# A new static order for one fused kernel: the first convolution block ahead of the second on every queue

## The chip, the cores and the metric

One NeuronCore of one Trainium2 chip runs the whole program. The metric is the device time of an execution in microseconds (us); smaller is better.

## The reference

```python
# x = A_q (2048 x 640), k = A_k, v = A_v
q   = layernorm(x)
ks  = sum over t in 0..3 of k shifted down by t rows * shift_k[:, t]      # a short causal filter
kv  = ks * v
y   = causal convolution of kv with ssm_k over the 2048 rows, per column  # by FFT, length 4096
h   = x + q * (y + kv * ssm_D)
z   = layernorm(h)
out = h + (silu(z @ w_gate) * (z @ w_up)) @ w_down      # 640 -> 1728 -> 640
```

All inputs and the output are bf16.

## The kernel before

**The work.** The 2048 rows are cut into four blocks of 512 rows, `j` = 0 to 3, and the 640 columns into two halves of 320, `c` = 0 and 1. Per block there is a convolution part and a feed-forward part. A convolution of length 1024 between blocks is done as matmuls with constant tables. For each block and half:

- `kvm`, `kva`, `kvv` (VectorE, L501): the four taps and the product with v.
- `s1X`, `s1K` (TensorE, L492): the first transform step of kv and of ssm_k, four groups `b` each, evacuated as `e1X`, `e1K` (L475 on ScalarE, L476 on VectorE).
- `shX`, `shK`: four transfers from SBUF to SBUF that regroup the partitions; they need all four `e1`.
- `s2X`, `s2K`: the second step, four groups `G`, evacuated as `e2X`, `e2K`. In block 0 three of the four spectra come in one dense step from a table of 1 MB (`full`) and need no `s1`, no `sh`.
- `swB`, `swX`, `swC`: transfers that swap even and odd partitions of a spectrum, two issues each.
- `mr`, `mi`, `ar`, `ai` (VectorE, L501): complex products of spectra, 1280 columns each. Block j uses the spectra of the blocks before it as well.
- `i2` (TensorE), `e3` (ScalarE L478 or VectorE L479), `rs` (transfers), `i1` (TensorE): the inverse. `i1` needs all four `rs` of its half.
- `o`, `h` (VectorE) and `q` (L777 on VectorE, L778 on ScalarE): the gate and the residual sum; then batch statistics `bn`, `ag` (L755, L759), `va` (L766), a power on GpSimd `nr` (L768) and `nm` (L770) for the second layer norm, in two pairs of row tiles.
- `hn`: the normalised rows; turned by TensorE in block 0 (`tr`, L988, evacuated by `te`) and by transposing transfers in the others (`hx`, L981).

Feed-forward: `gu` is a group of five matmuls of 512 columns (each of four groups in block 0's first pair as two of 256); `si` and `ue` on ScalarE (L1034, L1050) and `gm` on VectorE evacuate a pair; `dn` is the down projection, three groups for each of four row tiles; `fa` adds the residual and `st` stores.

So `s2K10G1` reads: second step, K, block 1, half 0, group 1. In `i1011` the step is `i1`, then come block 0, half 1 and row pair 1.

**The order.** All 1,219 operations are collected in a list. A table `_ORDER`, compressed and written into the source as text, gives each an engine and a start time, made offline from fixed costs per operation. `replay` sorts by these times and so fixes, for each of the five queues (TensorE, ScalarE, VectorE, GpSimd, SyncE "SP"), which operation follows which; `emit` then adds the semaphore waits. Each queue is worked in order. On the chip nothing waits for a start time, but the times have three more effects: rotating buffers are handed out in their order; the gaps that they leave on TensorE before the first `gu` are filled with matmuls of 192 columns on zeros (the fillers, L515, `o.lead`), one for each 0.083 us (0.166 in the first 6.9 us); and a transfer that would have nothing to wait for is tied to the last operation that ends before its start.

```python
gap = o.start - end - 0.25
o.lead = max(0, int(gap / 0.083)) if o.start > cold else max(0, int(gap / 0.166))
```

**Buffers that matter here.** PSUM has four tiles of two banks: `pF` (two) and `pC` (two); block 0's convolution uses both kinds, later blocks `pC` alone, and feed-forward `pF`. `H` (between `e3` and `rs`) has two buffers, `HT` (between `rs` and `i1`) one, `PP` (products) three, `KIN` and `VIN` one each. The weights `wg3`, `wg9` and others go into space that the table `full` had.

The memset `gpad` (`P.warm`) zeroes what the fillers read.

Of the kernel before, what the change touches and what calls it, by code (L numbers as in the profile page):

```python
# [1126 lines left out]
_ORDER = (
    "c-pO030PBC7A7x`kdOtkhwLj^$i4sx*~tb3LLh`B2#6?%vRJFFindy}X>Bc4i+qk&#tpYBE|t1f9c|UNRIS#PDq2NtYf-0)wiPG1b!_X@nXmV}@0|0_yZ4-X"
    "{`=ntfDi~2h=Dv101AQ+ofrrRg+M_F2!g;<1Ny{!v?eOi0Y3J@fe!=rsX+8CS|?^;*(3A&EKepr$4cnH3*^y$qG1pUjcz^qfDa5b=Fxyafafz&JzxOvH|k+p"
    "=(8~Rb*~`!4F7SPPj&WG6nNCi<CgwBIq>|+A%Bp30KJE^9(sQbQs9FzKnCD}dKOB+A2#)$jCcUbQ|x%=gkRfwUhMv~B=CQfjN%A9Mils~5Pity=Rowo@a|dU"  # L1130
    "co+vj$m1p;{~Lb5?+O5qejC4u1AoXr;0gbtr5>UM{HcBxPD^4UF)JaFm;qS?xdN$z@PP_|2|Ws70+sPCG2cU+z*t~DZ~?%BI`DWb1@<AN4^|IpM7g1#K@Y@)"
    "AR@@Su|2UII0|f!<Hvp!TM8D#uE1YMyoTsS-bT_<+tI^;4FC*U58Vr$4xRxqus$FH{SsuvB4Wd_T~HL*2X%vIW0%D?!M=kB;-<#M!>7Xc!kvimu%BUK#A!rx"
    "{I&SiNG^(xtVeD|DiKo<Y4KI@Juo*s2tNtm5Z{Dyqb{S==t*cMx*ok9U6Y_mIE&em5W=p-9mMWQ>`QFJ+`vx5y+b;OuY!4Fcfhc5)o~}|vf+#2TyQFQBX(C@"
    "ZfpSNMRX#zB9_EAz(=F^qF=!5z#tR*6S5NLB{sw%;RW%%@%xd3P!VJgQjZj)M<wpZl5v%|d)NZpIoxdAQT%OuKH(cefH;x39P1=ZBJL;FkhYSpl9mxS5V0f*"
    "X%gu?$wj_RT1mb|9zu?gH<GuJ&yh<g4U{&DFlkKEJxmvA5<W~_OJBeik&tW{OV8RT=w{Cn9TFWBy&-8%dV%^fC4*X?1X8zAI+J!%ebkw>9NIoAg1(k+rb`*k"
    "%#T=KbB;4;tWxemRu{KlP$BH)mk7=a>y!PW@k|QiJ8l;DF0+<*m-jJG#qSiJN-h_y7nO)5Y$zunTEl*ubCz>lBolukX_QvUa#df;7RvLLe)S%;RdGP^qjIcj"
    "s``j{M~XpqL_SNk1cr&P1PQ1%v@BsV;uNYEGlv2}Yccl|P?$+b7`2)X#qJ?rV|UQMrVr)n5!d1GAb9cT;<d;X$bRI@apSOOuu4oH=5S&S_7>WL5#Z+F|AAxR"
    "C!u@Lqfp0C0rYBg5vm2H#H_{CV>%Ot<6H0(2_1xK37ZmhiPIBz6TeJE5;JgYQVsbS?jZR(B_nA@5}PuT0#Ntk;|Ws2M8dp88TJ#xZNdS9gSeP_g=(hlOxjKf"
    "Qafk>y^B7UzMD>EjN@+QuHgK_q3~Yk>G%qvfe-Q*@vrcmf-M4Ja!Yb4W(9_vP?sP~+?JStos2z<XOl*fwvgtNgQPanb|Q>qrS40rr*Ecdar<xpQB7Qgi^1E7"
    "qlhojjHH`1CH)5)gRZ2N)21;tGgeY5v=F18v5O969$^k;-DY{&vw5TVSNS2{0iIBBn47};fZNNBVHL5KvhJ|P@;>5}@|UqU@#_S?@XrcblVQRm!V$@zCeIbV"  # L1140
    "B1Ve)M0Rnv*e}tf?2(j8Orj=9w`5t$MCmo@dKpnlmyVUzN#{z5vhU?@$XXPO<svypK3P6q{+_&2L02{@<|v8EpR}{J2K5)J3A*iSK`KZ4fo6ZICT)rKXqrkd"
    "*Zfm$PyZ@yo#v+gvSD|IK7(LhX}V~9*DSV1Qa{vvZWwI%HnlN>Yr2@eM9;IVvE&)n*)(>e=@ny#In#XHL^Ch5Fzl~p@*JS+kmrJ9gj4K-dC*xkR-p}-33rq_"
    "I$g8e*`8j{xojM^pIk;BLD|S+ayDppqz_7+lBP(P=(F{Bqt(=7xNahuTg|!nW_%oB0U>$?DPR(s`U<s~UC0^5+0E%>Q#gwmy^K1(fqRZyB)r6=vh2*!%u?q2"
    "%$Y0=dkuf7V3;6IykF2KIL7A-E(kQqPT|<-O}N2J5cMScl8c2`g>Q*);#T2&F<dfEGCk$1l!-E5%7T=ODW9h-lYT3qDoRrLQoZO!(H8L~ak;cz%9Q2FVr2G|"
    "ZL*UxhD<5{n|!3=o?^42P`O4KqpDD?RmG&vSCKTjv|TEh<_pa#?O^R(-Om=4^;=_{xzXBbZLq^LH(GC5-Nsc$hV8fwY45i0rPb5nj55Y1hL`z1%fvY^*e&8n"
    "u1HVI+GHeoSh7q~A&)4WYPw>Iyj{*$1QZVG80j$idBs6hf+|jZUwujmSM5|fR0}kE-3oQT_Pkc7ou<2}hO1xFbm>;70%;Ygp|tk2*z|Sj7=4?$R^Jgl!TISP"
    "!+rgGh7U5_M!$ZG9%EQ-kQ(cZ%QH@7+%jxU?J)8(YBTyXVl5F%lkt?X%v5ZC-+aSrw9T-otxK)ftPWeDv)i)K^_Fdndz{T_Uv9r{w`PvXJeS##>31y5?6ONU"
    "8y)Qqg7c!I)-lF`aypzf&d;6QQF+sq;L33tow=@K&b!VEm*2h0HN%Z?AMy?HHRPSin~`7PyPZES2bD9^+njqRr#g@1qj@p8Tm0Gnw{zbt$O<0ySh6zm+ww`-"
    "R)1Q-)WY6EZBc8{Yk@;SOR+lpldPWLgkVL^{9<H?Txcpd5a=tcEkp-q7P&(ohjSx`BB;88;=`d(SQPo9c6;QrlC08COW9?aC4oU*gGx)w%9b;IiosH@w8T0&"
    "ZG=~wzc=qfJ~7YjUsQO~uPzV;t^_bedy9T#zssR<=W;E)cHZCBH?<}WKXqN|;<PF0RXS&y#9+<Pm@b*OSza(rG2bvR)E(DxObbj4%~DIM^^RqyGsX6{WtW9)"  # L1150
    "t+wuW+;+enX^wq1n{%f--?PGVBI{>Yde-bLcJ^1<f}Hl8#o1T0wK*79o$IDk<?8TU_7FUo9-^l*yC$2K1A4>WCEjg0cf7f|K;9i+W`26!)Vy8!DaF%+C4r=("
    "#^UwG?$9^ICyGuK%?X?haDuJDW5Ic0vNl_nm)@OTr*AXOx7WDVn|f>$?ai*ATulzOv)vYNAD#1#N9XIyD{^<aN4Z<wYqHK{DLk)w1ld32Ov#se|K;W8-p>hm"
    "FXl9PC*-cqZOpr$+nE=W*Xq0FGv^ok=H>hRs|tQBI1%VBP!<x4@ctIR+`rJzEqJlO?c3qI=08yIgFm^jvCv$!uP`gHIB+X~4i*QO1T%wkgWbV<!HVM3#e&e-"
    "(5etDd^WT;bRmQdRfOc>Vc{L&OX1RRFpQ4872X)05Sbm7oe@I`Cz2GQl#GtFM4|^+(qGb1q8+5IY^~fmOkBkoy1MFm#k7j%DxiAQkk_iK%V(F7E7lCYT;5WF"
    "9y)%gYxu_DcZX_fEQ61hpRTU2-Zi*n_@E&NhWLkF8tSS1au~O4OX*K#OUqKrCYCjpvuZZgY#nK+ZK}-}v2TQTWamh3ZCc%~y3O^e4YL}OYuDAf>krm58~zP&"
    "9!w_"
)


# [26 lines left out]
```

## Time and profile before

| | |
|---|---|
| median of 11 runs | 312.33 us (307.07 to 315.2) |
| the profiled execution, its own time | 313.62 us |
| its span, first to last instruction | 311.8 us |
| TensorE, VectorE, ScalarE, GpSimd busy | 285.3, 235.0, 187.4, 27.0 us |
| mean granted TensorE clock | 0.986 |
| instructions | 4,974 |

A busy TensorE here includes the fillers, and a matmul's record is longer than the interval at which the next follows, since matmuls are pipelined. So busy time says how long the engine was not empty, and not how much work was done.

### The profile page before, as it was taken

To read this page: it belongs to the slowest core of one execution; us is meant where nothing else is said; L and a number is where in the kernel's file an instruction comes from. 1 tells how busy PE (TensorE), PEld (TensorE's weight loads), DVE (VectorE), ACT (ScalarE), POOL (GpSimd) and SP (SyncE) were. 2 spreads that over 40 slices of the span, in tenths; PEclk is the share of its full clock that TensorE was granted. 3 is DMA by queue.
4 is the path that set the end of the run, shared out by engine and by line. 5 is a ranking of instruction groups with operands and counts; after the bars stand their busy time and mean duration, and the time that the engine had idled before them with its cause. 6 is when DMAs were issued, how large, how long until landed. Compare 5 with 4: busy or idle time off the path is not lost.

```text
span 311.8 us, 4974 instructions
## 1 busy us (share of the span) xinstructions
PE 285.3 (91%) x1765; PEld 169.1 (54%) x1780; DVE 235.0 (75%) x406; ACT 187.4 (60%) x280; POOL 27.0 (9%) x34
## 2 busy tenths in 40 slices
...
GB/s 226 330 168 308 147 210 252 201 204 276 216 301 240 299 266 298 151 273 191 211 288 9 137 182 126 113 163 181 214 113 84 44 43 84 2 0 0 2 84 43
DMA packets 53116, 52.09 MB, mean 167 GB/s; under 512 B 21202, under 2 KB 46163, under 8 KB 53092
## 3 DMA queue, kind: packets, MB, share of 16 engines
...
q10 hardware_dynamic: 1010, 0.79, 0.7%
q8 instruction: 14, 0.23, 0.3%
q14 instruction: 10, 0.08, 0.1%
...
## 4 chain that ended last, share of the span: by engine, by line
PE 60%; DMA 15%; DVE 10%; ACT 7%; SPq 4%; issue 3%; POOL 0%; ACTq 0%; DVEq 0%
PE ps L492 56%; DMA sb<-sb 11%; DVE sb L501 8%; SPq L483 3%; ACT sb L475 3%; PE ps L515 3%; DMA sb<-in_A_ssm_k_dram 2%; ACT sb L778 1%; DMA sb<-in_A_q_dram 1%; DVE stt L755 1%; ACT sb L478 1%; ACT sb L790 1%; PE ps L624 1%; DVE sb L777 1%; POOL stt L768 0%
## 5 line engine op out<-in xcount | busy, mean ns | idle before, releaser
L492 PE MATMUL ps<-sb 128*128 128x320 bf16 (+3 forms) x1113 | 207.9, 337 | 2.7 <-DVE sb L501 1.5
L501 DVE TENSOR_TENSOR sb<-sb 128x1280 bf16<-128x1280 bf16 (+2 forms) x238 | 174.2, 768 | 17.3 <-PE ps L492 6.1
L492 PEld LDWEIGHTS ps<-sb 128*128 128x128 bf16 (+2 forms) x1128 | 109.0, 98 | 83.9 <-issue 5.4
L475 ACT ACTIVATE sb<-ps 128x640 bf16<-128x640 f32 x131 | 88.7, 712 | 39.0 <-PE ps L492 38.0
L492 PE MATMUL ps<-sb,tab 128*128 128x320 bf16 x450 | 79.8, 308 | 10.5 <-DMA sb<-sb 6.5
L492 PEld LDWEIGHTS ps<-sb,tab 128*128 128x128 f16 x450 | 42.9, 100 | 38.9 <-DMA sb<-sb 8.1
L501 DVE TENSOR_TENSOR sb<-ps,sb 128x640 bf16<-128x640 f32 (+3 forms) x34 | 29.2, 858 | 42.2 <-PE ps L492 40.4
L1034 ACT ACTIVATE sb<-ps 128x1024 bf16<-128x1024 f32 (+2 forms) x32 | 29.3, 916 | 23.7 <-PE ps L492 23.5
L478 ACT ACTIVATE sb<-ps 128x640 bf16<-128x640 f32 x31 | 21.1, 705 | 12.7 <-PE ps L492 12.6
L778 ACT ACTIVATE sb<-sb,stt 128x320 bf16<-128x320 bf16 (+1 forms) x34 | 24.0, 729 | 7.4 <-DVE stt L770 4.8
L515 PE MATMUL ps<-sb 128*128 128x192 bf16 x158 | 20.0, 275 | 7.7 <-ACT sb L475 4.9
L755 DVE BATCH_NORM_STATS2 stt<-sb 128x6 f32<-128x320 bf16 x48 | 22.3, 485 | 0.2
L1050 ACT ACTIVATE sb<-ps 128x1024 bf16<-128x1024 f32 x18 | 18.4, 1024 | 6.0 <-PE ps L492 5.1
L515 PEld LDWEIGHTS ps<-sb 128*128 128x128 bf16 x158 | 14.6, 108 | 13.2 <-ACT sb L475 7.9
L768 POOL TENSOR_TENSOR stt<-stt 128x2 f32<-128x2 f32 (+1 forms) x10 | 11.4, 1138 | 52.8 <-DVE stt L766 42.4
L476 DVE CAST sb<-ps 128x640 bf16<-128x640 f32 (+1 forms) x8 | 6.2, 780 | 9.1 <-PE ps L492 9.1
L804 POOL TENSOR_TENSOR stt<-stt 128x4 f32<-128x4 f32 x2 | 2.6, 1296 | 77.8 <-DVE stt L802 77.8
L790 ACT ACTIVATE sb<-sb 128x640 bf16<-128x640 bf16 x8 | 6.0, 744 | 2.4 <-DMA sb<-in_A_q_dram 2.4
L797 ACT ACTIVATE sb<-sb,stt 128x640 bf16<-128x640 bf16 x8 | 6.6, 832 | 0.0
L777 DVE TENSOR_SCALAR sb<-sb,stt 128x320 bf16<-128x320 bf16 (+1 forms) x14 | 5.5, 395 | 0.9 <-DMA sb<-sb 0.5
L483 POOL DMA_DIRECT2D sb<-in_B_w_down_dram x3 | 2.1, 698 | 33.1 <-DVE sb L501 29.1
L483 POOL DMA_DIRECT2D sb<-in_A_k_dram x2 | 2.1, 1028 | 27.8 <-DVE stt L759 27.8
...
## 6 DMA issues: line engine op xcount, KB each, us to landing
...
```

Source lines behind the costliest of these rows:

```text
L475: fns = {"act": lambda a: a.activation(out=dst(), in_=src(), func=ACTF.Copy), "dve": lambda v: v.tensor_copy(out=dst(), in_=src())}
L478: fns = {"act": lambda a: a.activation(out=dst(), in_=src(), func=ACTF.Copy, scale=scale), "dve": lambda v: v.tensor_scalar(out=dst(), in0 ...
L483: fns = [(lambda g, d=d, s=s: g.dma_start(d(), s())) for d, s in subs]
L492: return lambda t: t.matmul(o(), l(), r(), start=st, stop=sp)
L501: return lambda v: v.tensor_tensor(out=o(), in0=a(), in1=b_(), op=op)
L515: P.fill = lambda t, pt: t.matmul(B32(pt, 1, 192), V(GUT, 13 * 512 + 256, 128), V(GUT, 13 * 512, 192), start=True, stop=True)
L755: vec(dve1(CW, False), lambda v: v.bn_stats(st6(l, j, b, c), V(xt, b * D + c * CW, CW)), [(xt, (b, c))], [(ST, ("s", j % 2, b, c))], prio, ...
L768: P.op({"pool": 0.95}, lambda g: g.tensor_tensor(out=y, in0=va, in1=stt[:, 288:288 + hi - lo], op=ALU.pow), c1 + [(ST, "half")], c3, prio, ...
L778: "act": lambda a: a.activation(out=dst(), in_=src(), func=ACTF.Identity, scale=rs(l, j, b), bias=tmv(l, j, 3)[:, b:b + 1])},
L790: P.op({"act": act_c(D) + 0.22}, lambda a, b=b, jt=jt: a.activation(out=V(jt, 0, D), in_=V(xt, b * D, D), func=ACTF.Copy, accum_out=tmv(l, ...
L1034: P.op({"act": act_c(n)}, lambda a: a.activation(out=dst(), in_=src(), func=ACTF.Silu), rd, wr, -1000, name=f"si{j}{i}")
L1050: P.op({"act": act_c(1024)}, lambda a: a.activation(out=V(ut, 0, 1024), in_=B32x2(u, 512), func=ACTF.Copy), [(u, 0), (u, 1)], [(ut, 0)], - ...
```

## The change

The table is replaced by another; costs, operations, tiles and pools stay as they are. Besides, `replay` puts the memset `gpad` first on its queue (before, the memset `wpad`, 0.33 us, came first).

```diff
@@ -126,6 +126,11 @@
                 tl.left -= 1
                 if tl.left == 0 and tl.pool is not None:
                     self.pools[tl.pool].free.append((max(p.finish for p in tl.touch), tl.base, tl.touch))
+        q = self.order[self.warm.eng]
+        q.remove(self.warm)
+        q.insert(0, self.warm)
+        for i, o in enumerate(q):
+            o.pos = i
 
         end, cold = 0.6, 6.9
@@ -1125,35 +1130,34 @@
 _INFO = None
 _ORDER = (
-    "c-pO030PBC7A7x`kdOtkhwLj^$i4sx*~tb3LLh`B2#6?%vRJFFindy}X>Bc4i+qk&#tpYBE|t1f9c|UNRIS#PDq2NtYf-0)wiPG1b!_X@nXmV}@0|0_yZ4-X"
...
+    "c-pm730PBC7EWGPLKYGdLLhrW_JwSOY-Aw|Ss)}35)uU2Q3R!Kt#un)t75Ao)rt#R>8G{sj*41w7qw2uqS$KdI$CS(xK?YeI(CBEs%`z+nXhy1cJ6uS{^#8P"
...
```

Decoded, the two tables differ as follows (`xN` for N groups in a row; a convolution group is named by step and block alone). TensorE, from the sixth group of `s2K0` on to the first feed-forward groups:

```
before: ... i20x2 s2X0x2 s1X1x2 i20x2 s1X1x2 s1K1x2 i20 i10x2 s2X1 i20 s2X1x2 s1K1x2 i20x2 s1X1x2 s2K1x2 i10
        s2K1x2 s2X1 s1X1x2 i10 s1K1x4 tr00 i21 gu0x2 i21 tr01 gu0x6 s2X1 gu0 s2K1 gu0 i21 ...
after:  ... i20 s2X0 i20 s2X0x2 i20 s1X1 i20 s1X1x3 i20 i10 i20 i10 s2X1 i20x2 s1K1x3 i10 s1K1 i10 s2X1x3 s1X1
        s2K1 s1X1 s2K1 tr00 s2K1 gu0 tr01 gu0x4 s1X1 gu0x3 s1K1 s1X1 gu0 s2K1 gu0 s1K1 gu0 ...
```

Of block 1, `s2K10G2`, `s1X11b1`, `s1X11b3`, the four `s1K11` and `i210G1` stand ahead of the first `gu` before, and behind it after. On VectorE, thirteen instructions of the products and taps of blocks 1 and 2 and of statistics stand ahead of the second `nm` of block 0 before and behind it after (`mr1000`, `mr1001`, `mi1000`, `mi1001`, `ar1001`, `ai1001`, five of `kvm20` and `kva20`, `bn0130`, `ag013`); six come ahead of it (`he01`, `q013`, `bn0110`, `ag011`, `hn00`, `hn01`). SP begins `taps kin0 kraw00 x0 kraw01 full vin0 tab1` before and `taps kin0 kraw01 kraw00 full vin0 x0 tab1 shK00G0 tab2 kin10 swB000` after. The weights `wg3`, `wg9` and `wu3` are issued by GpSimd before, and after by SP, in the order `swB100 wu3 gul1 wg9 wg3 wu9`. 17 operations move from ScalarE to VectorE and 16 the other way; 22 transfers change their queue. At the end, TensorE has `i13x2` and eleven `dn2` ahead of the last stage before, and after `i13`, two `dn2`, `i13` and nine `dn2`. The last stage itself (27 `gu3`, 12 `dn3`) differs in the order within it. The fillers are 158 before and 176 after.

More of the change, by code (lines that the diff above doesn't have):

```diff
@@ L1127 @@
 _ORDER = (
-    "c-pO030PBC7A7x`kdOtkhwLj^$i4sx*~tb3LLh`B2#6?%vRJFFindy}X>Bc4i+qk&#tpYBE|t1f9c|UNRIS#PDq2NtYf-0)wiPG1b!_X@nXmV}@0|0_yZ4-X"
-    "{`=ntfDi~2h=Dv101AQ+ofrrRg+M_F2!g;<1Ny{!v?eOi0Y3J@fe!=rsX+8CS|?^;*(3A&EKepr$4cnH3*^y$qG1pUjcz^qfDa5b=Fxyafafz&JzxOvH|k+p"
-    "=(8~Rb*~`!4F7SPPj&WG6nNCi<CgwBIq>|+A%Bp30KJE^9(sQbQs9FzKnCD}dKOB+A2#)$jCcUbQ|x%=gkRfwUhMv~B=CQfjN%A9Mils~5Pity=Rowo@a|dU"
-    "co+vj$m1p;{~Lb5?+O5qejC4u1AoXr;0gbtr5>UM{HcBxPD^4UF)JaFm;qS?xdN$z@PP_|2|Ws70+sPCG2cU+z*t~DZ~?%BI`DWb1@<AN4^|IpM7g1#K@Y@)"
@@ L1132 @@
[L1132 to L1155, printed above, removed]
@@ L1156 @@
-    "9!w_"
+    "c-pm730PBC7EWGPLKYGdLLhrW_JwSOY-Aw|Ss)}35)uU2Q3R!Kt#un)t75Ao)rt#R>8G{sj*41w7qw2uqS$KdI$CS(xK?YeI(CBEs%`z+nXhy1cJ6uS{^#8P"
+    "o(Dj|U<d#LKWYF33I+9V;sXi=L!j{)3Opx}pS34v;w=vGRPX-)ebj$pi2L*(d$Rln$`i+*4d7p%1VGPb0RlhOAo0Ze1p<ZicL?Z-#4-NZ@+cSx1VDc=^<zR_"
+    "%)!%J#^ty5pRV~FC(l{IPp;B`^Jl|6eu}4nz;och9|Q;g8XOYeJ@$I6{V7aA9x(-pmjW1gH2qgBL7%M%=%ZqIwmM$u0Dxb_-Ty7*?=cz={^u|XeN@!{E2Gb+"
+    "{v!KN`~iQMzsCdt&j0~02mm}+f53BW0l#7k_}%$MJaqt3kT5>_TL<_mxDLD?JQs*T4g=MY5V{@oHP``+1S)}*z+~wAP&Z5i-vWLJy9A6#VnA4s2>3226{tiW"
@@ new lines @@
+    "MUIEhPN+h+qvj(*aC<^4T8!ah9M~A<FPO8~BS0Et6$F5Wp`SoAU}Ioz$P&mJs2<h^-2)v2eF*&$Iuf=Eb|1z^?1udt-ho()IE$Ez9G;Mhcz_fl;V3_9YT}7R"
+    "4*DWWlQ<!<2&qlbBG)DyLims<)SIY_sD#9mXeDMG<{;*E%qN&M?7y)?acEp0t}E#>9#4=YElzp`XT#6KuORdh_QKHcW$^p(0Add!6*&$07K8w;fwjOVB`{Fw"
+    "i5-a&^lJ1V)CSB0OgC1A+lkA?Eydlyjf7VsuE18ocP3s&zl{0;H5J*E)QY>G<ioe)dy<myQT%QE4*W{OeL^5Pk2pDb3Z9QIPJWm?jChI&CAAa3Pgavw5swh_"
+    "NM)o6Bw@;^6bZ>dT0we`bdXe*GA!lo6ghb;`5b01?pP{@9A->mY$HP{5Q2$(m^+ML#BLKBMVEx1l0QyuAfr?7rj(~HBF{-(N;#LBoi-_rn|_KCqAX26nl_4B"
@@ new lines @@
+    "NS{qRkp3>Um(HRgnDyL7-mHx4+yQ(7Z=&E1Gm|-w^%7$=%fs%<n8AUu*YPp@H11*HE23_?fVPQ!fw6@)iJ|4>32%yZ(oUIA#gU(vzmbVh98{f>E|A^IoUg#D"
+    "Od_RtjHFh2LU9$|k+2jALa)K|2`3YD1Qli%egm-@b2HIRo{s5G^^<5xiz)Z08B{OzJk6VMAGtkY7b=*zJduKKLsz0l5_S^K6Qs#-LLH$OFCuJ8zLm^M8J#=`"
+    "lZY+BPR6!jcViD?T-XByPy9tc!(SuOQijJ_d!4wEs7k6%YDf{1Hm88d7|MvWWt2l{D(ZM@1${8}8(If_HwBc|kaCsWn*3ohjHo7h)0UE?)b&&ZZ62+VHkN*m"
+    ";b6{WE@WO}x>>ilG)9Ee$#G=d%n0!xifS{|oZ~z;KO*QBj1ppH`Pg@`SFlzbH|b1LC1Fjnf;cPvWV$!)owRFdx^xJ|n8u<js8d+0sf&p>h`Fi5Q)iOSl5~_o"
@@ new lines @@
+    "l%doEX%}d)^fQc!Of|iR4x+2*7}_}6KbR-!=b6XoaCSR;1nV06VMa5L$5-=K@M`#dTw%sr>~6M^(a30F-(`=;uyMxlx;be6IR0K9PH<E}6SfKG3jQf57PbqI"
+    "i+V&!;-TVmVxq((St9a@w~67B?ULJ)F6kL*mt>9PisYgMC0!%kCk@EBGMXGNn;=^tdt0_urjgH=yX6^~%jNS_Fm<c)j`9ulWffSnKdUs$t7%a?wSU*NX1}AL"
+    "E6cKvX;&yuXLsvLOiK-)7$rt)j^7ltD78m52eTV>x3%T^Cc`B?MvpX)FxMM8EmN)XoINJ8rP{nOXS8{)Mc`cLEOzzeo%9qqPPrE3McfzMH!O#&LEDzx3Xdcg"
+    "VV`N=>|l95Pp+YKQdUrxvu3fkt2?z<vbO2`*?sz6^Ci>aoUz6kmJJrFwS}CVvM;rSa-EW#-jMzc?O)Vb#<C0+=L|=|9m~DP+02#kZe)DTn=j~Na#&%;`;02q"
@@ new lines @@
+    "QPy}Cmi>UUgY$!En}{m#3C8e2f;s$se2K73ctS9QXBK@akO~(GdE&X^%=jO-NmMJLN^4|mWpu?dDM{9*ydta2%#ulzM)_g6S1?sTljchg$nVGpXU@;;%v>T%"
+    "QIa!PWCj!$6eE>L)ehwV)h1P<`m|c0QD+e~HJXpJtJPc7?`iI8tXWiTlXa|hLC$RRe(OZr6gxS$#b&S_$>E!~*{<6-j^Pd+V+SLb+0GQRwzK@~;hauBLR2ey"
+    "Aetn;B$+1d6^caj6=e#$x>fb6qFK30uFQlemCAvNnF_eNSNT%bB=vaJYE_lWq28?dAS)-UIcr_k7L7z3)%0c6YS(D3**)2JwduOyy1TkD`h9whd7U0)7;bLW"
+    "FE?-v2IEb`=SIBIVk|QJXxL~ZnA(k>8K)ZyvtKj))yOt&G&Pz~ISX@&a%AR><^;=D3)K3N^)-vdI^Ei5(b~+pUpW`KGV?auuG;R{thuvt0egi#%f2PI&fc3V"
@@ new lines @@
+    "vahq>w<Dci$2t26`$ETUJH@fi@r9$#sdMgknw((g4Cfr@HmBV6sw>xZ-Sv{Iq;Q=7yMk#2kiaN^d!WtB^U?~&<WKf3D!}@0`3ilJU{CN+{@|jEA+vkGdrzS!"
+    ";PPAuGzS+I9SL-Y{GnK}v1Dt>hn@mYQy3i9d#{D}L{=ADiv=a)L-^2=(3tSPQeX7bXi4m1`RC#G2($Ey(t-iI%JK&E4hWXNUv7&XiUrG#m7Q)Pu@lrI#ai(u"
+    "`vcu8zV(Hi!g~cr{j^|G(dOc=;Qk_Ss3mkdgyaUe%eW7?O&Jv4etv7#F7<I8Tfa!F)2Ve6bj^mn288KH6UyQ+t+oDWwPr8LzHhFx7)&coZd;Fy=a^zUXBJsD"
+    "<zCO#xg>eJT{m4i`-(iAdu-kkH^STD1bf1sLT|SZk$<(|q1Wx}@U3)z;l?;OJ8Sc1=RL45a)iD0Zg0M-U}}Ne59IIg%+9}@&nO&O$O&Hd&ktM-RD{#RsA5~F"
```

4 lines of the change are left out of this document (added).

## The prediction

> **What bounds the kernel now.** I read the busy times by stage first, cut where the first matmul of each feed-forward stage starts and where the last convolution ends (columns: stretch, length, busy time and count of TensorE, weight loads, VectorE, ScalarE, GpSimd, then clock, DMA share, GB/s):
>
> ```profile
> 0.00:77.00 77.00, 63.62 (x447) 40.90 (x448) 57.17 (x106) 48.45 (x72) 12.43 (x19) 0.96 0.75 231
> 77.00:262.00 185.00, 177.60 (x1078) 104.52 (x1091) 165.29 (x289) 131.58 (x200) 14.53 (x15) 1.00 0.57 178
> 262.00:306.30 44.30, 44.09 (x244) 23.67 (x244) 11.75 (x13) 7.33 (x8) 0.00 (x0) 1.00 0.07 23
> ...
> 77.00:255.20 178.20, 170.93 (x1030) 99.87 (x1042) 163.22 (x285) 131.58 (x200) 14.53 (x15) 1.00 0.58 181
> ```
>
> Two resources are nearly full between 77 and 255 us: TensorE, and VectorE with 163.2 of 178.2 (15.0 idle). After 262 TensorE runs the last feed-forward stage alone. The slack lies ahead of 77, and there the busy figure misleads, because of the fillers:
>
> ```profile
> L515 PE MATMUL ps<-sb 128*128 128x192 bf16 x158 | 20.0, 275 | 7.7 <-ACT sb L475 4.9
> ```
>
> Next the issue rate. The last stage is 135 matmuls of 512 columns and 112 of 320 by the code, and takes 306.23 - 261.76 = 44.5 us by the chain of waits: 0.216 and 0.136 us each fit. At these rates (0.056 for a 128-column transpose) all 336 TensorE groups are 257.9 us of work. The last one ends at 306.2, so 48.3 us are not work. Ahead of the first feed-forward group, which ends at 77.7, lie 36.8 us of work with it: 40.9 of the 48.3 us are lost there. Only 7.5 us are lost later.
>
> Then the chain of waits and TensorE's timeline, to see what the front waits for:
>
> ```profile
> 26.51 0.61 SPq L483
> 27.12 0.04 issue
> 27.16 5.67 DMA sb<-sb
> 32.83 0.02 issue
> 32.86 0.84 DVE sb L501
> ...
> 60.89 5.21 DMA sb<-sb
> 66.10 0.05 issue
> 66.14 0.46 PE ps L492 x2
> ```
>
> ```profile
> 66.14 0.45 PE L492 MATMUL ps<-sb,tab 128*128 128x320 bf16 x2 [2.59 <-DMA sb<-sb]
> ...
> 74.92 0.73 PE L988 MATMUL ps<-sb 128*128 128x128 bf16 x10
> ...
> 76.98 1.26 PE L492 MATMUL ps<-sb 128*128 128x256 bf16 x10
> ```
>
> The pair at 66.14 is `s2K10G1`, of block 1. It stands in TensorE's queue ahead of block 0's last inverse group `i1011`, so block 0 waited for block 1's 5.2 us shuffle: `i1010` ended at 63.05, `i1011` only at 69.94. That is what the change takes apart. The transposes at 74.92 (`tr00`) and the first feed-forward matmuls follow from it.
>
> **What the Trainium skill says.** "TensorE: Matmul & The Clock Gate", Back-to-back issue gap: N/2.4 + 2.5 ns, so 215.8 and 135.8 ns; the stage above agrees within 0.5%. The same page's table of specifications gives ScalarE and VectorE a strict first-in-first-out queue: an instruction that waits holds all behind it; VectorE's 2.33 us before 67.36 is such a wait. "DMA: Bandwidth & Descriptors", Issuing engines are not separate DMA queues: moving a transfer between SP, ACT and POOL saves issue time alone, so I price the ten or so transfers that change queues in the front at their 0.4 to 0.6 us of issue. Its Anatomy of one DMA gives 2.0 us plus bytes over 436 GB/s, 2.4 us for 160 KB. The page's median for these shuffles is 2.3 us, but on the chain they take 4.7 to 5.7; I use those.
>
> **The change part by part.** No arithmetic is added; each operation keeps its size.
>
> *TensorE ahead of the first feed-forward group.* Seven groups of block 1 (`s2K10G2`, `s1X11b1`, `s1X11b3`, four `s1K11`) and `i210G1` move behind it: 26 matmuls of 320 columns, 26 x 0.136 = 3.5 us. Work with that group falls from 36.8 to 33.3. Fillers rise from 158 to 176 (18 x 0.083 = 1.5 us); they stand in front of groups that wait for data anyway and are free while that wait lasts, at most +1.5.
>
> *The front's chain*, old ends against mine:
> - Loads. `x0` goes behind `full` and `vin0`, and both `ktr` run together. The pair `s2K00G0/G1` lies at 10.4 us of work instead of 11.4 and `ktr01` waits for nothing. I put `e2K00G1` at 23.5 (before 26.15). The swap `swB000`, two issues of 0.6 and 5.7 us, lands at 30; `mi0000` ends at 30.7 (before 33.7).
> - `mi0010` follows after eleven VectorE instructions, 6.5 us: 37. `i200G3` ends at 38.3 (before 42.2), its evacuations at 39.8, the `rs00` transfers (0.6 each, 4.5) land at 44.5; `i1001` 45.6 (before 46.9).
> - HT and the two H buffers are single file: `rs01` can't start before `i1001` has read HT. `i201G2` then ends near 48.5 (before 56.3, held by `mi0110`, which came behind outputs and taps on VectorE); its evacuations wait for H until 51.5; the last `rs01` lands at 56.
> - `i1010`, `i1011`: 56.1 and 57.2, with nothing of block 1 that waits between them (before 63.05 and 69.94).
> - VectorE: `o010` to the first `nm10`, 17 instructions, 5 us: 62.0, the GpSimd power of 1.2 us beside the batch statistics. Then `hn00`, `hn01` on VectorE (0.45 each), 63.1; second half 65.1.
> - Ahead of `tr00` TensorE still has `s2K10G1` and `s2K10G0`, whose shuffles are issued after `e1K10b1` (57.3) and land at 63 to 64. So `tr00` 65, `te00` (1.2 us on ScalarE) 66.3, first feed-forward group **67** instead of 77.7.
>
> TensorE's loss at that point: 67 - 33.3 = 33.7 instead of 40.9, 7.2 us won.
>
> *Beside the first feed-forward stage.* New costs: weight piece `wg3` was on GpSimd, issued at 60.0; now it is on SP behind `swB100`, `wu3`, `gul1` and `wg9`: about 2 us of issue after `e2K10G0`, plus 4.6 us landing, near 73.5. `gu011` needs it after 6.6 us of work, at 73.6: 0 to 2 us, I take 1. VectorE's `e1X11b1` (behind four half-groups on TensorE) costs VectorE up to 3 us near 68.
>
> TensorE's bound for the last stage: 67 + (213.4 - 33.3) work + 7.5 + 1 = 255.6, against 261.7: 6.1 won.
>
> *VectorE's bound.* Thirteen instructions of blocks 1 and 2 (8.8 us) are behind the second `nm10`'s place now, six others ahead of it. By its own intervals VectorE has done 51.4 us when the second normalisation begins, instead of 57.7; from there to the last `nm13` the new order has 171.1 us, the old one 162.7 (2 us of the difference are evacuations taken over from ScalarE). So 64.6 + 171.1 + idle. Idle was 15.0; a reason to gain: block 0's chain no longer interrupts; a reason to lose: more to do beside feed-forward evacuations. Bounds 11 to 20; I take 16, with `e1X11b1` in it: 251.7. From the last `nm13` (255.2) to the landing of the last `hx3` took 5.2 us before: 256.9.
>
> *The end.* After `i1311` nine groups of the third down projection remain, instead of eleven: 11.4 us of cover, 13.9 before. The chain below it (`y`, `o`, `h`, statistics, power, `hn33`, two transposing transfers of 1.23 us issue, 2.4 landing) was 12.4; with `hn31` earlier I make it 10.5. It fits by 1 us; if not, 1 to 2 us go back.
>
> The later bound counts: 256.9 against 261.7, **4.8 us** won, on the profiled execution 313.6 - 4.8 = 308.8. That execution lay 0.4% above the median of 312.33; in the same ratio, 312.3 x 308.8/313.6 = **307.5 us**.
>
> **The rivals.**
> - *VectorE gives nothing back* (no change). Idle of 20 us cancels it: 64.6 + 171.1 + 20 + 5.2 = 260.9. For it: VectorE is at 92% already and got 8.4 us more behind the front. Against: ScalarE has 47 us of idle there. Time 311.5 to 312.
> - *VectorE becomes the bound and loses* (slower). One mechanism: first-in-first-out on VectorE while it evacuates block 1's groups that TensorE reaches only between feed-forward groups. With idle of 26 the last stage starts at 266.9: 5.2 later, 317.5 us. It decides from 19.6 us of idle on as a loss, and from 24 as one over 1%.
> - *The front is bound by transfers anyway.* Six shuffle or swap hops of 4.7 to 5.7 us are 31 us of the front. If the `rs` and `sw` hops don't move up, the first group comes at 73.5, TensorE's loss is 40.2, and nothing is won: 312.
> - *The front's gain holds in full*: VectorE idle 11 or less and the first group at 64: TensorE's bound 252.5, 9 us won, 303.
>
> **How the numbers follow.** Forecast (gain of 2.5 to 7): 0.40; full gain: 0.17; no change by either way: 0.23; slower: 0.20. A difference of 1% (3.1 us) is about what a measurement of this kernel can tell from none. Faster 0.57, same 0.23, slower 0.20. The range goes from the full gain with a little more, 301.5, to the beginning of the slower case, 316.5: about 0.08 of the slower one lies above it, 0.05 below. The likeliest case alone is 305 to 310.
>
> **What would show it.** Right: the first 256-column matmuls near 67; fillers x176; no gap on TensorE between the two `i101` groups; TensorE's loss by then under 35 us; VectorE done with the last `nm13` near 252; the last stage from 257. Wrong: a start of the first feed-forward group after 72; a stall of over 2 us at `gu011`; VectorE idle over 20 us between the first feed-forward group and the last `nm13`; a wait of the last stage's first matmuls on the transposing transfers.

## The result, and the profile after

| | before | after |
|---|---|---|
| median | 311.32 us of 42 runs (307.07 to 315.38) | 315.22 us of 11 runs (314.32 to 317.58) |
| ratio | | 1.0178, 95% interval 1.0149 to 1.0207 |
| the profiled execution, its own time | 313.62 us | 315.54 us |
| its span | 311.8 us | 313.7 us |

The changed kernel is slower, by 1.3 to 1.8%; 307.5 was forecast. The ratio leaves out runs over 1.5% above the fastest of their kernel, which are many of before's (it spreads over 8 us, and the profiled execution is one of them) and none of the changed kernel's (3 us): so it says 1.8% where the medians of all runs stand at 315.22/311.32 = 1.0125. The two profiled executions differ by 1.9 us only.

The stages of the changed kernel, cut as before (stretch, length, busy time and count of TensorE, weight loads, VectorE, ScalarE, GpSimd, clock, DMA share, GB/s):

```profile
0.00:77.00 77.00, 62.39 (x482) 43.46 (x483) 54.44 (x106) 42.79 (x62) 9.02 (x16) 0.93 0.69 218
77.00:262.00 185.00, 176.53 (x1050) 101.61 (x1061) 167.45 (x289) 137.48 (x209) 16.75 (x19) 1.00 0.61 184
262.00:310.00 48.00, 45.79 (x255) 24.89 (x256) 12.84 (x13) 7.33 (x8) 0.00 (x0) 1.00 0.08 27
```

VectorE has 2.7 us less behind it at 77 us than before and 2.2 more in the stretch after. The table of groups has the fillers as counted in the source:

```profile
L520 PE MATMUL ps<-sb 128*128 128x192 bf16 x176 | 20.3, 268 | 6.1 <-ACT sb L480 4.9
```

(The lines of the changed kernel are 5 higher than those of before.) Its chain of waits in the front (start, length, what):

```profile
5.20 5.96 DMA sb<-cst_ident
11.16 0.14 issue
11.29 2.72 PE ps L629 x24
...
60.01 0.25 issue
60.26 1.26 PE ps L497 x8
...
63.50 5.19 DMA sb<-sb
68.69 0.05 issue
68.74 0.46 PE ps L497 x2
```

Two things are to be seen. At 11.16 TensorE got `ident`, the identity that its first transposes `ktr00` and `ktr01` multiply by: a wait that the chain of before does not have. And at 68.69 a 5.2 us shuffle ends the wait of `s2K10G1`, as at 66.10 before; but what stands behind it is another group now. TensorE's timeline (start, length, line, operation, count, idle before and its releaser):

```profile
60.26 1.25 PE L497 MATMUL ps<-sb,tab 128*128 128x320 bf16 x8 [1.54 <-DMA sb<-sb]
...
68.74 0.72 PE L497 MATMUL ps<-sb,tab 128*128 128x320 bf16 x4 [0.46 <-DMA sb<-sb]
69.98 0.59 PE L520 MATMUL ps<-sb 128*128 128x192 bf16 x5 [0.52 <-ACT sb L480]
70.40 0.43 PE L497 MATMUL ps<-sb,tab 128*128 128x320 bf16 x2
70.67 0.72 PE L993 MATMUL ps<-sb 128*128 128x128 bf16 x10
...
72.76 0.72 PE L497 MATMUL ps<-sb 128*128 128x256 bf16 x5 [0.61 <-ACT sb L480]
```

The eight matmuls at 60.26 are `i1010` and a group of block 1, `s1K10b1`, whose evacuation starts that shuffle; `i1011` ends at 62.40, against 69.94 before. So the change did free block 0's inverse, by 7.5 us. But `tr00` (L993) stands at 70.67 behind the pair at 68.74, and the first feed-forward group ends at 73.5, only 4.2 us earlier than before, with 3.5 us less work done by then.

On VectorE, beside the first feed-forward stage:

```profile
71.44 0.45 DVE L782 TENSOR_SCALAR sb<-sb,stt 128x640 bf16<-128x640 bf16 x1 [1.58 <-PE ps L993]
...
76.53 0.82 DVE L481 CAST sb<-ps 128x640 bf16<-128x640 f32 x1 [2.05 <-PE ps L497]
...
82.06 3.88 DVE L506 TENSOR_TENSOR sb<-sb 128x1024 bf16<-128x1024 bf16 x5 [0.88 <-ACT sb L1039]
```

It waited for a buffer that `tr00` had to free, then for `s1X11b1`, which TensorE has between feed-forward groups, then for a silu.

The account that the rest leans on is the prediction's: the time at which a group ends less the work of all groups up to it, at 0.216 us a matmul of 512 columns and 0.136 of 320. It is TensorE's loss, and it can be read where the first feed-forward group of blocks 0, 1 and 2 ends, and at the last matmul. One profile of each kernel:

| kernel | order | first group ends | loss there | block 1's first | block 2's first | end |
|---|---|---|---|---|---|---|
| before | old | 77.7 | 40.9 | 45.7 | 48.4 | 48.3 |
| b1 | old | 77.2 | 40.3 | 44.6 | 47.7 | 47.7 |
| e6 | old | 79.8 | 43.0 | 48.3 | 51.3 | 51.2 |
| e7 | old | 72.8 | 35.9 | 41.1 | 44.2 | 44.1 |
| e11 | old | 77.9 | 41.0 | 45.8 | 52.3 | 52.3 |
| e13 | old | 74.6 | 37.8 | 42.9 | 45.9 | 45.9 |
| e14 | old | 74.3 | 37.5 | 42.7 | 44.5 | 44.5 |
| after | new | 73.5 | 40.2 | 47.5 | 49.9 | 50.1 |
| e1 | new | 71.9 | 38.6 | 46.2 | 49.9 | 50.1 |
| e4 | new | 69.8 | 36.5 | 42.3 | 48.4 | 48.6 |
| e5 | new | 70.5 | 37.2 | 45.3 | 47.9 | 48.1 |
| e8 | new | 70.7 | 37.4 | 43.6 | 45.4 | 45.6 |
| e9 | new | 74.1 | 40.8 | 48.7 | 50.5 | 50.7 |
| e10 | new | 71.1 | 37.8 | 45.7 | 49.7 | 49.9 |
| e12 | new | 72.0 | 38.7 | 45.5 | 45.4 | 45.8 |

The front of a single profile is not known well. e7 and e13, and e8 and e12, have the same front and lie 1 to 2 us apart at the first group. Before and e7 differ by the place of `gpad` alone and have level medians, and yet lie 5 us apart there: before's profiled execution took 313.6 us and e7's 309.4. The stages after the front repeat better, so they carry more of what follows.

### The profile page after: what moved, and what is told of

Same layout as the page of the kernel before. It is cut to its first block, busy times and chain, and to the rows that moved or that the text cites. A ratio compares the mean times of both kernels' runs of the same rounds, so it can differ in the third digit from the quotient of the medians.

```text
span 313.7 us, 5002 instructions
## 1 busy us (share of the span) xinstructions
PE 284.7 (91%) x1782; PEld 170.0 (54%) x1798; DVE 234.7 (75%) x407; ACT 187.6 (60%) x279; POOL 25.8 (8%) x35
## 4 chain that ended last, share of the span: by engine, by line
PE 71%; DMA 13%; ACT 6%; DVE 3%; issue 3%; SPq 2%; ACTq 0%
PE ps L497 67%; DMA sb<-sb 8%; ACT sb L480 4%; PE ps L520 3%; SPq L488 2%; DVE sb L506 2%; DMA sb<-in_B_w_up_dram 2%; DMA sb<-cst_ident 2%; DMA sb<-in_A_q_dram 2%; PE ps L629 1%; ACT sb L1039 1%; DVE sb L481 1%; ACT sb L783 0%; ACTq L488 0%; ACT sb L483 0%
## 5 line engine op out<-in xcount | busy, mean ns | idle before, releaser
L497 PEld LDWEIGHTS ps<-sb 128*128 128x128 bf16 (+3 forms) x1128 | 108.6, 98 | 83.9 <-issue 3.5
L480 ACT ACTIVATE sb<-ps 128x640 bf16<-128x640 f32 x132 | 90.3, 720 | 49.8 <-PE ps L497 42.7
L506 DVE TENSOR_TENSOR sb<-ps,sb 128x640 bf16<-128x640 f32 (+3 forms) x34 | 29.2, 858 | 42.8 <-PE ps L497 38.6
L1039 ACT ACTIVATE sb<-ps 128x1024 bf16<-128x1024 f32 (+2 forms) x32 | 29.3, 915 | 24.4 <-PE ps L497 24.3
L783 ACT ACTIVATE sb<-sb,stt 128x320 bf16<-128x320 bf16 (+1 forms) x33 | 22.7, 709 | 4.7 <-DVE stt L775 3.1
L520 PEld LDWEIGHTS ps<-sb 128*128 128x128 bf16 x176 | 16.1, 107 | 11.2 <-ACT sb L480 7.9
L760 DVE BATCH_NORM_STATS2 stt<-sb 128x6 f32<-128x320 bf16 x48 | 21.4, 480 | 0.1
L773 POOL TENSOR_TENSOR stt<-stt 128x2 f32<-128x2 f32 (+1 forms) x10 | 9.4, 941 | 61.1 <-DVE stt L771 48.3
L782 DVE TENSOR_SCALAR sb<-sb,stt 128x640 bf16<-128x640 bf16 (+1 forms) x15 | 6.0, 410 | 2.6 <-PE ps L993 1.6
L809 POOL TENSOR_TENSOR stt<-stt 128x4 f32<-128x4 f32 x2 | 2.6, 1304 | 52.3 <-DVE stt L807 52.3
L488 POOL DMA_DIRECT2D sb<-in_A_k_dram x3 | 3.1, 1018 | 43.1 <-DVE stt L760 43.1
L629 PE MATMUL ps<-sb 128*128 128x128 bf16 x24 | 2.7, 309 | 2.9 <-DMA sb<-cst_ident 2.9
```

Of the source, the lines that this page charges most:

```text
L480: fns = {"act": lambda a: a.activation(out=dst(), in_=src(), func=ACTF.Copy), "dve": lambda v: v.tensor_copy(out=dst(), in_=src())}
L488: fns = [(lambda g, d=d, s=s: g.dma_start(d(), s())) for d, s in subs]
L497: return lambda t: t.matmul(o(), l(), r(), start=st, stop=sp)
L506: return lambda v: v.tensor_tensor(out=o(), in0=a(), in1=b_(), op=op)
L520: P.fill = lambda t, pt: t.matmul(B32(pt, 1, 192), V(GUT, 13 * 512 + 256, 128), V(GUT, 13 * 512, 192), start=True, stop=True)
L760: vec(dve1(CW, False), lambda v: v.bn_stats(st6(l, j, b, c), V(xt, b * D + c * CW, CW)), [(xt, (b, c))], [(ST, ("s", j % 2, b, c))], prio, ...
```

## The experiments

Each kernel was timed in 5 rounds against the kernel before on the same chip. Ratios are to it, with 95% intervals, formed as above. The medians of all runs of the same rounds give ratios that lie up to 0.5% lower or 0.3% higher; where that matters they are given too.

**b1: the kernel before, once more.** No edit.

> The kernel before, unchanged, for a second profile of it (the first was of an execution at 313.6 us, above the median of 311.3) and for the width of a difference of nothing. Both theories: ratio 1.000, within 0.5%. If a typical execution is at 311, its loss of TensorE ahead of the first feed-forward group should be 1 to 2.5 us under the 40.9 us of the first profile, or its later loss under 7.5 us: which of the two tells where the kernel's own spread comes from.

1.0032 (0.9977 to 1.0088), median 311.97; by the medians 0.9997. In the profile the loss at the first group is 40.3 again, and 7.4 us come later.

**e1: the load of `ident` early.** The new table, with one start time changed:

```diff
  ScalarE's queue
- shm tap1 tap0 ident he02 tab0 ...
+ shm ident tap1 tap0 he02 tab0 ...
```

> The new order, with the load of the identity moved on ScalarE's queue from behind tap1 and tap0 to right behind shm. Theory F (the front is late for its own reasons: the identity landed at 11.2 us and both ktr waited for it, and block 1's s2K10 groups stand ahead of tr00): ktr00 ends near 10 instead of 12.75, the first feed-forward group comes 1 to 3 us earlier than 73.5, and the whole is 1 to 3 us shorter, 312.5 to 314. Theory L (the order beside the feed-forward stages costs the time, and the front is swallowed there): the front moves, the end stays at 315.

1.0111 (1.0055 to 1.0167), median 314.42, against 1.0178 (1.0149 to 1.0207). `ident` was issued at 1.13 and landed at 6.01; `ktr00` ended at 10.8 instead of 12.75 and the first feed-forward group 1.6 us earlier. That is about a third of the loss, and by the medians as well (1.0076 instead of 1.0125); the two intervals overlap a little.

**e6: the same edit the other way round, in the old table.**

```diff
  ScalarE's queue
- shm tab0 ident tap0 tap1 ...
+ shm tab0 tap0 tap1 ident ...
```

> The kernel before, with the load of the identity behind tap0 and tap1 on ScalarE's queue, as the new order has it. ktr00 ends 1 to 3 us later than 9.6. Theory V: the front of the kernel before has the same chain, so VectorE's idle at the second nm10 grows by 1 to 2 us and the whole by about 1 us (ratio 1.002 to 1.006). Theory D: no change.

1.0106 (1.0038 to 1.0174), median 315.21. Over b1 that is 0.7%, of the size that e1 gave back; here too the intervals overlap. TensorE's waits in the first 20 us (waited for: us in total, times, longest), for this kernel and then for the changed one:

```profile
PE ps L624 <- DMA sb<-cst_ident: 4.2, 1, 4.2
```

```profile
PE ps L629 <- DMA sb<-cst_ident: 2.9, 1, 2.9
```

The load is 32 KB. `ident` stands behind an activation (`tap0`, `tap1`) on the queue that issues it; what delays it is that place.

**e2, e3: the two tables cut and joined at the first `gu`.** e2 has the new order up to the first `gu` and the old order for what is left; e3 the reverse.

> The new order up to the first feed-forward group, the order of before for all operations behind it. Theory F: the front is what lost, so this stays near 315. Theory L: the front is even (TensorE had lost 40.2 us at the first feed-forward group, against 40.9), so with the old order behind it the time is that of before, 310 to 312.

> The order of before up to the first feed-forward group, the new order for all operations behind it. Theory F: the time of before, 311 to 312. Theory L: the new order's losses come back, 2.5 us or more over before, 314 to 315.

e2: 1.0219 (1.0149 to 1.0289). e3: median 318.06, runs from 312.16 to 320.69, and no ratio (1.0193 by the medians). Both are slower than either parent, which no theory had. The seam is why, at least in e2: `tr00` ended at 72.3 and the first `gu` only at 82.4, for what the new order had put behind the first `gu` now came ahead of it. They don't separate the front from the rest.

**e4: the transposes ahead of block 1's waiting pair.** e1, and in TensorE's queue (their evacuations likewise):

```diff
- s2K10G1 s1X11b2 s2K10G0 tr00 ...
+ tr00 s2K10G1 s1X11b2 s2K10G0 ...
```

> The new order with the identity's load early, and with tr00 and te00 ahead of block 1's s2K10G1, s1X11b2 and s2K10G0 (and their evacuations) on TensorE and ScalarE. Theory V (VectorE has a fixed 220 us of work ahead of the last nm, and its idle time sets the end; the new order brings block 0 forward without giving VectorE less idle time, and idles 8.5 us instead of 3.4 beside the first feed-forward stage): hn03's wait of 1.6 us on tr00 goes, the first feed-forward group ends near 70 instead of 71.9, the whole is 1 to 2 us under the kernel with the identity early alone, 312.5 to 313.5. Theory D (what is won ahead of the first feed-forward stage is lost again at later waits on transfers): stays at 314 to 315.

1.0146 (1.0087 to 1.0206), no better than e1 (by the medians 1.0093 and 1.0076). Yet the front moved. In TensorE's timeline `tr00` starts 5.6 us earlier than in the changed kernel:

```profile
65.04 0.72 PE L993 MATMUL ps<-sb 128*128 128x128 bf16 x10
```

and the loss when block 1's first group ends is 42.3, 5.2 less. Not all of the front's part is the edit's. Of the 5.6 us, 3.2 were there at `i1011`, where e4 and e1 have the same queues and e4's profile is 1.5 us ahead of e1's. From `i1011` to `tr00` e4 takes 6.6 us and e1 9.2, but from `i1011` to the first feed-forward group 10.6 and 11.3, for that group still stands behind groups of block 1. So the edit is worth over 2 us at `tr00` and some 0.6 us at the first group.

The gain was given back in the next stage, 6.1 us from block 1's first group to block 2's. ScalarE's timeline and TensorE's show where:

```profile
159.00 0.74 ACT L795 ACTIVATE sb<-sb 128x640 bf16<-128x640 bf16 x1 [3.08 <-DMA sb<-in_A_q_dram]
```

```profile
160.79 2.19 PE L497 MATMUL ps<-sb 128*128 128x512 bf16 x5 [2.42 <-ACT sb L1039]
```

The first is a step of the first layer norm of block 2, which waits for the load `x2`; the silu that has to free a bank of PSUM stands behind it on ScalarE. `x2` overwrites what block 0's stores `st0` read, and those stand behind shuffles in SP's queue.

**e5: two evacuations off VectorE.** e4, with `e1X11b1` and `e1K11b0` on ScalarE.

> The one before, and the two evacuations e1X11b1 and e1K11b0 back on ScalarE as in the kernel before. Theory V: VectorE's waits of 2.05 and 0.74 us for these two go and 1.5 us of work with them, so 2 to 4 us less again: 309 to 311.5, level with the kernel before or under it. Theory D: 313 to 315, no difference from its neighbour.

1.0147 (1.0096 to 1.0199): the same as e4. The waits of VectorE from 66 to 141 us, in e4 and then in e5:

```profile
DVE sb L506 <- ACT sb L480: 2.3, 2, 1.7
DVE sb L506 <- ACT sb L1039: 0.9, 1, 0.9
```

```profile
DVE sb L506 <- ACT sb L480: 3.6, 2, 1.8
DVE sb L506 <- ACT sb L1039: 3.2, 2, 2.8
```

ScalarE waited for the block 1 groups in VectorE's stead, what stands behind them on ScalarE came later, and VectorE waited longer for that: for silus (L1039) and other evacuations (L480). The loss from the first group to block 1's first rose from 5.8 to 8.1 us.

**e8, e9, e10: the stores and `x2` earlier.** In SP's queue `st03` and `st00` follow right after `hx12`, `st01` and `st02` stand further ahead, and on GpSimd `x2` goes ahead of `vin30`. e8 is e4 with this; e9 is the changed kernel with this alone; e10 is e1 with this.

> The kernel with the identity early and the transpose first, and with the stores of block 0 right behind their sums on SP (before: up to 6 us later, behind shuffles) and the load of x2, which needs their buffer, ahead of vin30 on GpSimd. Theory X (the first stage's gain is lost at x2: it landed at 158 to 163 us whatever the front did, ScalarE stands at l0s2 until then, feed-forward pair 2 is not evacuated and TensorE waits up to 3.5 us at gu121): x2 lands before 153, the wait at gu121 goes, 2 to 4 us under the kernel without this, 310.5 to 312.5. Theory D (other waits take its place): x2 lands early, the end stays within 1 us, 314 to 315.

> The new order with block 0's stores and x2 early, and nothing else. Theory X: x2 lands near 153 instead of 163, TensorE's wait of 1.0 us at gu121 and ScalarE's 2.0 us at l0s2 go: 1 to 2 us under the new order, 313 to 314.5 (ratio 1.006 to 1.012). Theory D: 315, ratio 1.015 to 1.018.

> The new order with the identity early, and block 0's stores and x2 early, without the transpose first. Theory X: the identity's 1 to 2 us and x2's add up: 311.5 to 313.5 (ratio 1.000 to 1.007). Theory D: as with the identity alone, 314.4, ratio 1.011.

e8: 1.0115 (1.0078 to 1.0152). e9: 1.0241 (1.0177 to 1.0306). e10: 1.0136 (1.0067 to 1.0205). By the medians they stand at 1.0142, 1.0225 and 1.0153. In all three the wait for `x2` is gone, and another is there, for a shuffle that the same queue now issues later. TensorE's timeline of e8:

```profile
154.94 0.45 PE L497 MATMUL ps<-sb,tab 128*128 128x320 bf16 x2 [1.74 <-DMA sb<-sb]
```

That is `s2X21G0`; in e9 it waited 1.57 us and in e10 2.18. So the wait for `x2` is where e4's gain went in its profile, but to free it brought nothing that is clear of noise: e8 and e4 overlap, and the two ways of forming the ratio order them differently. Nor does it make the changed kernel slow: there its time is taken by another wait as soon as it is freed.

**e11: `x2` late, in the old table.** The stores `st0` stand behind the swap `swC210` on SP, past up to six shuffles and swaps, and `x2` moves from SP to GpSimd, behind `vin30`.

> The kernel before, with block 0's stores behind shk30 and swC210 on SP, and x2 on GpSimd behind vin30, about as the new order has them. x2 lands 2 to 4 us later than 158.3. Theory X: 1 to 2 us over the kernel before, ratio 1.003 to 1.007. Theory D: no change, within 0.3%.

1.0202 (1.0147 to 1.0258). ScalarE's wait grew, and TensorE's timeline has it at the next evacuation:

```profile
163.22 0.74 ACT L790 ACTIVATE sb<-sb 128x640 bf16<-128x640 bf16 x1 [5.56 <-DMA sb<-in_A_q_dram]
```

```profile
164.69 0.72 PE L492 MATMUL ps<-sb,tab 128*128 128x320 bf16 x4 [3.02 <-ACT sb L475]
```

The loss from block 1's first group to block 2's is 6.5 us instead of 2.7: a place in a queue alone can cost the old order as much as the whole change did (1.0177 by the medians).

**e7: the memset `gpad` first, in the old table.** The code hunk of the change without its table.

> The kernel before with the one change of code alone: gpad first on VectorE's queue. The fillers start 0.4 us earlier and the tap groups with them; ktr waits for its load at 8.4 us anyway. Both theories: ratio 1.000 within 0.4%.

0.9965 (0.9932 to 0.9998), with medians of 311.63 and 311.70 in the same rounds: nothing or up to 0.7% faster (0.9998 by the medians). `tab0` and `ident` were issued 0.4 us earlier. This part of the change is not what costs.

**e12, e13: block 0's stores on GpSimd.** e12 is e8, e13 is e7, with `st00` to `st03` (in e13 `x2` too) taken off SP's queue:

```diff
- dma([...], 164, xc2, [], -900, name=f"st{j}{b}")
+ dma([...], 164, xc2, [], -900, name=f"st{j}{b}", eng=("sp", "pool"))
```

> The kernel of e8_transpose_first_x2_early with one edit: the four stores of block 0 are issued by GpSimd instead of SP, so that SP's queue beside the second feed-forward stage holds only shuffles and swaps (and GpSimd's holds stores, x2 and vin30). Theory 'SP's queue is the choke': what e8 left, the 1.9 us wait of VectorE for s2X21G0 behind shX21G0, goes; TensorE's loss at the end of the second stage falls from 45.4 to 43 or 44 us and the ratio to before from 1.0115 to between 1.000 and 1.006. Theory 'no single queue, each freed wait gives way to the next': another wait of 1 to 2 us takes its place in the same stage; loss 45 to 47, ratio 1.008 to 1.015.

> The kernel of e7_before_gpad_first with the four stores of block 0 and x2 issued by GpSimd instead of SP, in the old order. Theory 'SP's queue is the choke': before has the same stores in the same queue, its loss in the second stage (3.1 us from dn1 to gu2 in e7) falls by 1 to 2 us, ratio 0.988 to 0.993. Theory 'each freed wait gives way to the next': 0.994 to 1.000. If GpSimd's queue delays the power of the layer norm or vin30: 1.000 to 1.006.

e12: 1.0083 (1.0052 to 1.0114), by the medians 1.0034. The wait of `s2X21G0` is gone, without one in its place in the stage of block 1; a wait of `gu120` ahead of it is larger than in e8 (1.33 us and 0.21). TensorE's timeline:

```profile
144.64 1.02 PE L497 MATMUL ps<-sb 128*128 128x512 bf16 x4 [1.33 <-DVE sb L506]
...
154.96 0.43 PE L497 MATMUL ps<-sb,tab 128*128 128x320 bf16 x2
```

From block 1's first group to the end e12 loses 0.3 us, the least of all kernels here, and e8 2.0. Still it ends at 45.8, and e8 at 45.6: up to block 1's first group e12's profile had lost 1.9 us more, 1.3 of it in the front, where the two have the same queues. e13: 1.0034 (1.0001 to 1.0068), by the medians 1.0003, no gain over e7 and perhaps a loss; with 3.0 us lost in that stage, as in e7, the old order isn't held by SP's queue there.

**e14: the core of the change alone, in the old table.** e7, with block 0's last inverse group and its gate ahead of block 1's waiting group:

```diff
  TensorE
- s2K10G1 s2X10G3 s1X11b1 s1X11b3 i1011
+ i1011 s2X10G3 s2K10G1 s1X11b1 s1X11b3
  VectorE
- h010 mr1000 bn1001 bn1011 ... o011 ... h011
+ h010 o011 h011 bn1001 mr1000 bn1011 ...
```

`e2X10G3` also comes ahead of `e2K10G1` on ScalarE, and the fillers are 165 instead of 158.

> The kernel of e7_before_gpad_first with the core of the change alone: the last inverse group i1011 of block 0, and o011 and h011 behind it, stand ahead of block 1's s2K10G1, e2K10G1 and mr1000; all else is in the old order. If the wait of i1011 behind block 1's shuffle was on the path that sets the first feed-forward group, as the prediction had it: i1011 ends 4 to 6 us earlier than in e7 (64.6), first feed-forward group 2 to 4 us earlier than 72.8, and half of it or more is left at the end: ratio 0.984 to 0.992. If the freed time is taken by the next wait on VectorE and TensorE (block 1's groups s1K11 and the normalisation stand where they stood): i1011 earlier, first feed-forward group within 1.5 us of e7's, ratio 0.993 to 1.000. If block 1's delayed spectrum costs more than that: 1.000 to 1.008.

0.9926 (0.9890 to 0.9962), median 310.25 against 312.16 in the same rounds (0.9939): the fastest kernel here, and one that beats both before and after. How much of this is the swap and how much `gpad` is not settled: against e7 it is 0.4% by the ratios, whose intervals overlap, and 0.6% by the medians.

Its profile does not show where the gain is. `i1011` ended at 62.1, 2.5 us earlier than in e7 although its first transposes came 1.3 us later. But `tr00` did not move up. VectorE's timeline says why:

```profile
65.61 0.83 DVE L506 TENSOR_TENSOR sb<-sb 128x1280 bf16<-128x1280 bf16 x1 [0.71 <-ACT sb L480]
...
69.05 0.16 DVE L775 TENSOR_TENSOR stt<-stt 128x2 f32<-128x2 f32 x1 [0.17 <-POOL stt L773]
```

The first is `mr1000` of block 1. It needs the same shuffle that `i1011` was freed from, and it still stands ahead of block 0's second layer norm on VectorE. The second is that norm's first `nm10`: it ended 8.0 us after `i1010`, and 8.1 in e7, so nothing was won there. (The changed kernel, which has `mr1000` behind the norm, takes 6.1.) The rest of the way to `tr00`, by TensorE's timeline and ScalarE's:

```profile
69.92 1.74 PE L520 MATMUL ps<-sb 128*128 128x192 bf16 x19
71.53 0.73 PE L993 MATMUL ps<-sb 128*128 128x128 bf16 x10
```

```profile
67.64 2.22 ACT L480 ACTIVATE sb<-ps 128x640 bf16<-128x640 f32 x3 [0.74 <-PE ps L497]
69.76 1.72 ACT L783 ACTIVATE sb<-sb,stt 128x640 bf16<-128x640 bf16 x2
```

The normalised rows `hn00` and `hn01` (L783) are ScalarE's in the old order; they waited another 0.5 us behind three evacuations of block 1, and TensorE filled the time with fillers. The first feed-forward group ended at 74.3, against 72.8 in e7, and at the end the two profiles have lost the same (44.5 and 44.1 us).

## Why the prediction was wrong

The mechanism that the change was priced for is real in part: the last inverse group `i1011` waited for a shuffle of block 1, and no longer does. But the prediction let the transposes follow from `i1011`, and by data they don't. `tr00` turns the first pair of row tiles, which needs `i1000` and `i1010`. In the kernel before, that shuffle held it by way of VectorE's queue: `mr1000`, which waits for the same shuffle, and `o011` stand ahead of the first `nm10` there. (VectorE's 2.33 us before 67.36, which the prediction quotes, is the wait of `mr1000`.) e14's profile shows it from the other side: with `i1011` free and `mr1000` where it was, ahead of the norm, `tr00` gained nothing. In the new table `mr1000` is behind it and `i1011` follows `i1010` at once (62.4 after 61.0), so what counts is `i1010`; it moved from 63.05 to 61.0 only, where 56.1 was forecast.

So the step that failed is the front's chain up to `i1010` and on to `tr00`: it was priced at 67 us for the first feed-forward group and took 73.5. Of these 6.5 us, 4.9 were there at `i1010`, and 1.5 came at the pair ahead of `tr00`. A second term was mis-sized, the 8.5 us lost behind that group, which were 9.9.

*Loads, the first step of the front's chain: wrong.* The step took `ktr00` and `ktr01` to run with their data and put `e2K00G1` at 23.5. It looked at SP's queue alone. Every DMA of a step that is moved counts, those on ScalarE's queue too: `ident` had moved behind the activations there, was issued at 5.2 instead of 2.0, and `ktr00` ended at 12.75 instead of 9.86. `e2K00G1` came at 26.8, later than before. e1 and e6 show this step from both sides, at about 0.7% each with overlapping intervals; in e1's profile it is worth 2.0 us at `ktr00` and 1.4 at `e2K00G1`. What else made `e2K00G1` late was not separated.

*The hops of the front: too short.* From 3.3 us at `e2K00G1` the error fell to 1.2 at `mi0000` (31.9 for 30.7), and then rose to 3.0 at `mi0010`, 3.5 at `i200G3`, 5.3 at `i1001` (50.9 for 45.6) and 4.9 at `i1010`. The hop to `i1001` holds 1.8 us of it: its shuffle took 5.2 us where 4.5 were allowed, and TensorE ran at half its rate from 48.5 us on (shown below), which is another 1.1 us by an estimate from the intervals there. No gap opened between the two `i101`, as forecast.

*Ahead of `tr00`: seen, and mis-timed.* The prediction named the pair behind block 1's shuffles, and put their landing at 63 to 64. The shuffle was issued at 62.8 and landed at 68.7, mostly because `e1K10b1` was as late as `i1010` (62.3 for 57.3). `hn01` ended at 68.0 for 63.1, `tr00` at 71.4 for 65. By e4 to move the pair away wins over 2 us at `tr00` and about 0.6 at the first group. The first group ended at 73.5, not 67; TensorE's loss there was 40.2, where 33.7 was forecast and 40.9 was before. The rival "the front is bound by transfers anyway" had named just these, 73.5 and 40.2, in part by luck: it let no swap and no `rs` move up, while the products behind the swap came 1.8 us and `i1010` 2.1 us earlier, and it knew nothing of `ident`.

*Behind the first group: the loss is larger, not equal.* The prediction took over the 7.5 us lost later and added 1 for `wg3`. The measured term is 9.9, so 73.5 + 180.1 + 9.9 = 263.5, where the last stage did start; 255.6 was the sum forecast for TensorE and 256.9 the later bound. `wg3` cost 0.6 us. The rest is the first stage: from its first group to block 1's, the seven kernels in the old order lose 4.3 to 5.3 us, and the four in the new order that leave its transposes where they were lose 7.3 to 7.9 (after, e1, e9, e10). The slower rival's mechanism fits this: evacuations of block 1's groups, which TensorE reaches only between feed-forward groups, hold all that is behind them in a queue that is worked in order. VectorE idled 8.5 us between the second layer norms of blocks 0 and 1, and 3.4 in b1. But that it makes the difference is argued and not shown. e5 took two of these evacuations off VectorE, and the loss there grew: the wait went along to ScalarE. No single wait carries it; e4, with the transposes ahead, has 5.8 in that stretch.

*VectorE's bound.* 64.6 + 171.1 + 16 = 251.7 was forecast for the last `nm13`; measured, 69.4 + 169.7 + 18.0 = 257.1. The start is 4.8 us of the 5.4. The idle time of 18.0 lies between the forecast's 16 and the 19.6 from which the slower case was said to decide. (The prediction's own sum gives 261.7 - 5.2 - 235.7 = 20.8 for that point.) The "2 us of evacuations taken over" were not there: VectorE's work is about 220 us in both kernels.

*The end: right.* The last stage follows the down projection without a wait, on nine groups of cover.

*From the profile to the median.* The forecast scaled by 312.3/313.6. But before was profiled in one of its longer executions and the changed kernel in a typical one (315.54 against 315.22), so of the 3.9 us between the medians the two profiles show only 1.9. The granted clock goes with before's spread: of its 119 executions timed beside the experiments, the 16 with a mean clock of 0.994 or more took 309.7 us on average, and the 18 under 0.982 took 314.0. In before's profile the record has TensorE at half clock from 33.7 to 37.2 and from 67.9 to 71.3 us, in that of e7, with nearly the same queues, nowhere between 11.1 us and the end of TensorE's work. The changed kernel's six executions at 0.994 or more took 315.1 on average: at a like clock it is 1.7% behind. Why some executions fall into such stretches was not tested.

What stays open: with `ident`, transposes, `x2` and stores all mended (e12) the new order is still 0.3 to 1.1% behind before. The account puts it into the first feed-forward stage (6.8 us there, 5.2 in e7 and e14), in waits of at most 1.3 us each. Which rearrangement of that stage would remove them was not tried.
